# Linear attention into an MoE layer on one core: q, k and x transposed by DMA instead of on TensorE

## The chip, the core and the metric

The kernel runs on one core of a Trainium2 chip. The core has TensorE (PE, matmuls; its weight loads are counted apart as PEld), VectorE (DVE), ScalarE (ACT), GpSimd (POOL) and SyncE (SP). Each engine works through its own instructions in order, and waits on semaphores for the others. DMAs are issued from the queues of SP and POOL and run on 16 DMA engines that all queues share. TensorE writes to PSUM, and what it wrote there is read by DVE or ACT; SBUF is the large on-chip memory.

The metric is the device time of one execution, in microseconds. Before the change three runs gave 448.0, 448.2 and 449.42 us, median 448.2.

## The reference

The inputs are q, k and v of shape (8 batches, 8 heads, 576 positions, 64), a feature matrix w_phi (64 x 128), and the weights w_in (512 x 2048) and w_out (2048 x 512), all float32.

```python
def phi(x):
    proj = np.einsum('bhsd,df->bhsf', x, w_phi)
    proj = proj - np.max(np.abs(proj), axis=-1, keepdims=True)
    return np.concatenate([np.exp(proj), np.exp(-proj)], axis=-1)
q_p, k_p = (phi(q), phi(k))
kv = np.einsum('bhsf,bhsd->bhfd', k_p, v)
z = np.sum(k_p, axis=2)
num = np.einsum('bhsf,bhfd->bhsd', q_p, kv)
den = np.einsum('bhsf,bhf->bhs', q_p, z)[..., None] + 1e-06
attn = num / den
# heads side by side: x has 4608 rows of 512
h = x @ w_in
g = np.where(h > 0.0, h, np.exp(np.minimum(h, 0.0)) - 1.0)
out = g @ w_out
```

## The kernel before

**Attention.** The work is cut into 16 quads: quad i is batch i // 2 and four of its eight heads. For a quad, 128 partitions hold positions; the 576 positions of a head are 4 x 128 plus a tail of 64, and the tails of two heads share one block, so that k of a quad is nine blocks of 128 x 128 in bf16. `transposes` (lines 127 to 148) turns the nine blocks of k, and then those of q, on TensorE: eight into one PSUM tile `tr` (line 135), copied to `kT` or `qT` at once (line 137), and the tail block into `trt` (lines 139, 140). `project` (line 156) multiplies kT or qT by w_phi and takes the largest absolute value on DVE (line 164); `k_head` takes the exponentials `EK` on ACT (line 177); `k_scale` and `v_scaled` build `vs`, the scaled v, on POOL (lines 188 to 202; on DVE for quad 1); `q_features` makes `Eq` on ACT (lines 211, 219); `kv` accumulates kv (lines 252, 264); `out_head` and `out_tail` make numerator and denominator in `tot` (lines 285 to 324); `divide` writes `x` in bf16 on POOL (line 333). `x_out` (lines 340 to 362) transposes x on TensorE, again nine blocks, and copies them on DVE to `xT`, the tile of the batch's MoE chunk, and to `xT_tail`, which gathers the tails of all batches.

**MoE.** The 4608 rows are nine chunks of 512: chunk b is the main part of batch b and needs the x of quads 2b and 2b+1; chunk 8 (`B`) is made of all tails. A chunk is 16 units of `mm1` (four matmuls into `ph`, line 389, then exp on ACT, line 397, a subtraction of one on POOL, line 399, and min/max into `gT` on DVE, line 402) and four units of `mm2` (16 matmuls into `po`, line 410, a copy to `o_sb` on ACT, line 418, and a store issued from SP, lines 421 and 425). `o_sb` has two buffers.

**Order of the work.** The main loop has slots n = 0 to 16. `slot_steps(n)` mixes the steps of quad n (`new`: k, scale, q, vs, qf), of quad n - 1 (`old`: kv, out, x) and the transposes of quad n + 1 (`nxt["tr"]`), in an order written by hand. After each step MoE units are put in until their number reaches `due`, which grows evenly: 136 units over 14.5 slots, from slot 2.5 on (line 558). `chunk_ready` opens a chunk; for chunks 1 to 7 that is the last step of an even slot, right behind `old["x"]`. Units that are left at the end run behind the loop, with chunk 8. The instructions of an engine then stand in an order that a scheduler derives from this one; an instruction of a later step can stand ahead of one of an earlier step on the same engine.

**Loads and queues.** k and q come in from HBM through POOL's queue, cast to bf16 on the way (line 104 of `load_main`, and `load_tails`); v comes through SP's queue from batch 1 on. Tiles k_b, q_b and v_b have two buffers each, one for a batch; kT, qT, EK and Eq have two buffers each, one for a quad. Weights w_in and w_out come through POOL's queue in the first slots. SP's queue thus holds v loads and output stores, in order; a DMA that waits for its semaphores holds all behind it.

Of the kernel before, what the change touches and what calls it, by code (L numbers as in the profile page):

```python
# [9 lines left out]
BF16 = mybir.dt.bfloat16  # L10
# [12 lines left out]
def kernel(  # L23
# [10 lines left out]
    nc = tc.nc  # L34
    P = 128

    B, H, S, D = q.shape
# [6 lines left out]
    N_CT = DM // P  # L44
    N_JT = DFF // P
    CHUNK = 512
# [3 lines left out]
    TAIL = S - MAIN  # L50
# [3 lines left out]
    consts = ctx.enter_context(tc.tile_pool(name="consts", bufs=1))  # L54
# [13 lines left out]
    ident = consts.tile([P, P], BF16)  # L68
# [15 lines left out]
            out=w_out_sb[:, jt:jt + 2, :], in_=w_out_r[:, jt:jt + 2, :]  # L84
        )

    xT_tail = consts.tile([P, N_CT, B * TAIL], BF16)
    xTs = {B: xT_tail}


    HW = NT * D
# [31 lines left out]
    def attention_steps(i):  # L123
        b, qd = divmod(i, 2)
        st = states[i] = {}

        def transposes(n):
            src = kqv[b][n]
            m0, t0 = 4 * qd * HW, BW + qd * P
            nm = ("kT", "qT")[n]  # L130
            dst = st[nm] = work.tile([P, NS, P], BF16, name=nm)
            tr = apsum.tile([P, 8, P], BF16, name="tr", tag="ap")
            for j in range(8):
                o = m0 + j * P
                nc.tensor.transpose(tr[:, j, :], src[:, o:o + P], ident)  # L135
            copy = nc.scalar.copy if n == 1 and b == 0 else nc.vector.tensor_copy
            copy(dst[:, 0:8, :], tr)  # L137
            trt = apsum.tile([P, P], BF16, name="trt", tag="ap")
            nc.tensor.transpose(trt, src[:, t0:t0 + P], ident)
            copy(dst[:, 8, :], trt)  # L140
            if n == 0:
                st["m_k"] = small.tile([P, 2 * NS], FP32, name="m_k")
                st["EK"] = work.tile([P, 4, 2, NT * F], BF16, name="EK")
                st["EKt"] = work.tile([P, 2, 2 * F], BF16, name="EKt")
            else:
                st["m_q"] = small.tile([P, 2 * NS], FP32, name="m_q")
                st["Eq"] = work.tile([P, 2, 2, 2, 4 * P], BF16, name="Eq")
                st["Eqt"] = work.tile([P, 2, 2 * P], BF16, name="Eqt")
# [189 lines left out]
                )  # L338

        def x_out():  # L340
            tr = apsum.tile([P, 8, P], BF16, name="tr", tag="ap")
            for j in range(8):
                nc.tensor.transpose(
                    tr[:, j, :],
                    st["x"][:, j].rearrange("p c d -> p (c d)"),
                    ident,
                )
            if qd == 0:
                xTs[b] = xtp.tile([P, N_CT, CHUNK], BF16, name="xT")
            nc.vector.tensor_copy(  # L350
                xTs[b][:, 2 * qd:2 * qd + 2, :],
                tr.rearrange("p (s t) n -> p s (t n)", s=2),
            )
            trt = apsum.tile([P, 2, TAIL], BF16, name="trt", tag="ap")
            nc.tensor.transpose(
                trt.rearrange("p s j -> p (s j)"),
                st["x"][:, 8].rearrange("p c d -> p (c d)"),
                ident,
            )
            nc.vector.tensor_copy(  # L360
                xT_tail[:, 2 * qd:2 * qd + 2, b * TAIL:(b + 1) * TAIL], trt
            )

        def each(f, *a):
            return lambda: f(*a)
# [18 lines left out]
    def mm1(ch, jt):  # L384
        if jt == 0:
            gTs[ch] = gpool.tile([P, N_JT, CHUNK], BF16, name="gT")
        ph = mpsum.tile([P, CHUNK], FP32, name="ph", tag="mp")
        for ct in range(N_CT):
            nc.tensor.matmul(  # L389
                ph,  # L390
                w_in_sb[:, ct, jt * P:(jt + 1) * P],
                xTs[ch][:, ct, :],
                start=(ct == 0),
                stop=(ct == N_CT - 1),
            )
        e_sb = moesm.tile([P, CHUNK], FP32, name="e_sb")
        nc.scalar.activation(e_sb, ph, ACT.Exp)  # L397
        u_sb = moesm.tile([P, CHUNK], BF16, name="u_sb")
        nc.gpsimd.tensor_scalar(  # L399
            u_sb, e_sb, -1.0, 1.0, op0=ALU.add, op1=ALU.mult  # L400
        )
        nc.vector.scalar_tensor_tensor(  # L402
            gTs[ch][:, jt, :], u_sb, 0.0, ph, op0=ALU.min, op1=ALU.max
        )
# [47 lines left out]
    def chunk_ready(ch):  # L452
        first.extend((ch, jt) for jt in range(N_JT))

    def slot_steps(n):
        old, new, nxt = quads.get(n - 1), quads.get(n), quads.get(n + 1)
        if n == 0:
            return (
                new["k"] + new["scale"] + new["q"][:2] + nxt["tr"] + new["q"][2:]
                + new["vs"] + new["qf"]  # L460
            )
        if n == 1:
            steps = new["k"] + new["scale"] + old["kv"]
            for j in range(5):
                steps += new["q"][j:j + 1] + old["out"][j:j + 1]
                steps += new["vs"][j:j + 1]
            return steps + new["vs"][5:] + new["qf"] + nxt["tr"]
        if n == 2:

            return (  # L470
                old["kv"] + quads[0]["x"] + old["out"] + old["x"]
                + [lambda: chunk_ready(0)]
                + new["k"] + new["scale"] + new["q"] + new["vs"] + new["qf"]
                + nxt["tr"]
            )
        none = {"k": [], "q": [], "scale": [], "qf": [], "vs": []}
        new = new or none
        kk, qq, vv = new["k"], new["q"], new["vs"]
        steps = (
            old["kv"][:1] + kk[:1] + old["kv"][1:] + kk[1:3]  # L480
            + old["out"][:1] + kk[3:4] + old["out"][1:2] + kk[4:]
            + new["scale"]
            + old["out"][2:3] + vv[:1] + qq[:1] + old["out"][3:4] + vv[1:2]
            + qq[1:2] + old["out"][4:] + vv[2:3]
            + qq[2:4] + vv[3:4] + qq[4:]
        )
        for j in range(5):
            steps += new["qf"][j:j + 1] + vv[4 + j:5 + j]
        if nxt:
            steps += nxt["tr"]  # L490
        steps += old["x"]
        if n % 2 == 0:
            steps.append(lambda: chunk_ready(n // 2 - 1))
        return steps

    make_identity(nc, ident)
    for b in range(2):
# [18 lines left out]
    def load_kq(b):  # L516
        return [
            lambda f=f, n=n: f(n)
            for n in range(2)
            for f in (  # L520
                lambda n: load_main(nc.gpsimd, n, b, 0, 8),
                lambda n: load_tails(nc.gpsimd, n, b),
            )
        ]

    def load_v(b, after=None):
        if after is not None:
# [11 lines left out]
        f()  # L539
    extra = w_in_loads[3:] + load_kq(1) + w_out_loads  # L540

    UNITS = 136
    done = 0
    for n in range(NQ + 1):
        if n + 1 < NQ:
            quads[n + 1] = attention_steps(n + 1)
        if n % 2 == 0 and 1 < n // 2 + 1 < B:
            alloc_batch(n // 2 + 1)
            extra += load_kq(n // 2 + 1)
            load_v(n // 2 + 1)  # L550
        steps = slot_steps(n)
        for j, step in enumerate(steps):
            step()
            if n == 1 and step is quads[1]["scale"][0]:
                load_v(1, after=states[1]["em"][:, 0, 0:1])
            if extra and ((n == 0 and j > 16) or n == 1 or j % 3 == 2):
                extra.pop(0)()
            due = (n + (j + 1) / len(steps) - 2.5) * UNITS / 14.5
            while done < due and (first or second):
                moe_unit()  # L560
                done += 1
    chunk_ready(B)
    while first or second:
        moe_unit()
# [30 lines left out]
```

## Time and profile before

| | |
|---|---|
| median of three runs | 448.2 us |
| the profiled execution's own time | 447.22 us |
| span of its records | 445.4 us |
| mean granted TensorE clock | 0.977 |
| TensorE busy | 396.4 us, 89% |
| DVE busy | 283.8 us, 64% |
| ACT busy | 264.6 us, 59% |
| POOL busy | 243.8 us, 55% |
| HBM read / written | 36.77 MB / 9.44 MB |

The profile is of one execution. Its times count from the start of the span. Busy time is the union of an engine's instructions, and matmuls overlap, so a busy TensorE need not be at its peak. In the slices each digit is the busy share of 1/40 of the span in tenths; PEclk is the granted clock, DMA the mean busy share of the 16 DMA engines. A group is named by its line, engine and operation, with output <- inputs. In a list of waits, "A <- B" says that A's engine stood idle until B had ended. Some records of matmuls are missing: of 576 each, 556 of line 410 and 542 of line 389 are there.

### The profile page before, as it was taken

To read this page: it belongs to the slowest core of one execution; us is meant where nothing else is said; L and a number is where in the kernel's file an instruction comes from. 1 tells how busy PE (TensorE), PEld (TensorE's weight loads), DVE (VectorE), ACT (ScalarE), POOL (GpSimd) and SP (SyncE) were. 2 spreads that over 40 slices of the span, in tenths; PEclk is the share of its full clock that TensorE was granted. 3 is DMA by queue.
4 is the path that set the end of the run, shared out by engine and by line. 5 is a ranking of instruction groups with operands and counts; after the bars stand their busy time and mean duration, and the time that the engine had idled before them with its cause. 6 is when DMAs were issued, how large, how long until landed. Compare 5 with 4: busy or idle time off the path is not lost.

```text
span 445.4 us, 8463 instructions
## 1 busy us (share of the span) xinstructions
PE 396.4 (89%) x3194; PEld 221.5 (50%) x3248; DVE 283.8 (64%) x602; ACT 264.6 (59%) x585; POOL 243.8 (55%) x355
## 2 busy tenths in 40 slices
PE   3668659999999998999899989999889998999995
PEld 2445336555555455646465646554545454444442
DVE  2675859954897279927994589656978564443420
ACT  2854288745966487737775578566767733344331
POOL 9676078744694279446945494618283725342320
PEclk9955999999999999999999999999999999999999
DMA  8999929312830191119121912100000010011013
GB/s 135 215 186 233 227 28 106 107 49 58 98 107 25 71 108 55 55 71 132 23 86 56 145 28 83 48 25 25 2 0 25 25 42 32 24 50 47 25 47 71
DMA packets 45081, 33.12 MB, mean 74 GB/s; under 512 B 13904, under 2 KB 39632, under 8 KB 45040
## 3 DMA queue, kind: packets, MB, share of 16 engines
q0 software_dynamic: 28544, 14.82, 24.8%
q1 hardware_dynamic: 16496, 17.76, 12.9%
q8 instruction: 25, 0.41, 0.4%
q14 instruction: 16, 0.13, 0.1%
HBM read 36.77 MB, written 9.44 MB: 104 GB/s over the span
## 4 chain that ended last, share of the span: by engine, by line
PE 54%; ACT 14%; DVE 13%; POOL 11%; issue 5%; DMA 1%; POOLq 0%; ACTq 0%
PE po L410 24%; PE ph L389 13%; ACT EK L177 5%; ACT Eq L219 5%; POOL u_sb L399 4%; POOL vs L202 4%; PE pk L156 4%; DVE gT L402 4%; PE pkv L252 3%; PE tr L135 3%; ACT e_sb L397 2%; POOL x L333 2%; DVE m_q L164 2%; DVE m_k L164 2%; PE pn L285 2%
## 5 line engine op out<-in xcount | busy, mean ns | idle before, releaser
L399 POOL TENSOR_SCALAR u_sb<-e_sb 128x512 bf16<-128x512 f32 x144 | 87.7, 616 | 114.8 <-ACT e_sb L397 104.6
L389 PE MATMUL ph<-xT,w_in_sb 128*128 128x512 bf16 x480 | 130.5, 379 | 8.8 <-DVE gT L402 6.9
L410 PE MATMUL po<-w_out_sb,gT 128*128 128x512 bf16 x556 | 134.5, 379 | 0.8
L402 DVE SCALAR_TENSOR_TENSOR gT<-u_sb,ph 128x512 bf16<-128x512 bf16 x144 | 96.8, 681 | 56.8 <-POOL u_sb L399 56.2
L397 ACT ACTIVATE e_sb<-ph 128x512 f32<-128x512 f32 x144 | 86.4, 636 | 35.5 <-PE ph L389 33.0
L202 POOL TENSOR_TENSOR vs<-v_b,em 128x512 bf16<-128x512 f32 (+1 forms) x90 | 73.0, 830 | 27.4 <-ACT em L188 27.3
L410 PEld LDWEIGHTS <-gT 128*128 128x128 bf16 x576 | 54.5, 98 | 56.6 <-issue 1.0
L389 PEld LDWEIGHTS <-w_in_sb 128*128 128x128 bf16 x576 | 52.2, 97 | 52.3 <-issue 14.2
L219 ACT ACTIVATE Eq<-pq 128x512 bf16<-128x512 f32 x128 | 65.9, 639 | 15.5 <-PE pq L211 15.4
L177 ACT ACTIVATE EK<-pk 128x512 bf16<-128x512 f32 x128 | 68.0, 630 | 11.5 <-DVE m_k L164 11.2
L418 ACT COPY o_sb<-po 128x512 f32<-128x512 f32 x36 | 21.3, 593 | 83.9 <-PE po L410 66.7
L164 DVE TENSOR_REDUCE m_k<-pk 128x4 f32<-128x512 f32 (+1 forms) x80 | 49.0, 632 | 19.1 <-PE pk L156 18.7
L164 DVE TENSOR_REDUCE m_q<-pk 128x4 f32<-128x512 f32 (+1 forms) x80 | 49.4, 626 | 16.2 <-PE pk L156 16.0
L285 PEld LDWEIGHTS <-Eq 128*128 128x128 bf16 x512 | 30.2, 99 | 26.3 <-issue 10.5
L333 POOL TENSOR_TENSOR x<-tot,rec 128x576 bf16<-128x576 f32 x30 | 33.8, 1145 | 10.0 <-DVE rec L330 9.8
L285 PE MATMUL pn<-kv,Eq 128*128 128x65 bf16 x512 | 34.6, 196 | 4.9 <-DVE tot L295 1.1
L156 PE MATMUL pk<-w_phi_both,qT 128*128 128x256 bf16 x144 | 29.1, 288 | 4.4 <-ACT EK L177 2.2
L156 PE MATMUL pk<-w_phi_both,kT 128*128 128x256 bf16 x144 | 28.5, 287 | 3.2 <-ACT Eq L219 1.9
L295 DVE TENSOR_TENSOR tot<-pn,w 128x260 f32<-128x260 f32 x64 | 27.1, 424 | 5.6 <-PE pn L285 5.2
L137 DVE COPY kT<-tr 128x1024 bf16<-128x1024 bf16 x16 | 11.0, 688 | 29.8 <-PE tr L135 29.8
L301 DVE TENSOR_TENSOR tot<-tot,pn 128x260 f32<-128x260 f32 x64 | 26.7, 418 | 0.3
L252 PE MATMUL pkv<-vs,EK 128*128 128x65 bf16 x512 | 22.9, 198 | 1.9 <-ACT EK L177 1.2
(62 smaller groups left out, 358.8 us busy)
## 6 DMA issues: line engine op xcount, KB each, us to landing
out_dram<-o_sb SPq DMA_DIRECT2D x32, 256.0 KB, 2.3
v_b<-in_v_dram SPq DMA_DIRECT2D x7, 1024.0 KB, 5.7
k_b<-in_k_dram POOLq DMA_DIRECT2D x7, 512.0 KB, 6.9
q_b<-in_q_dram POOLq DMA_DIRECT2D x7, 512.0 KB, 7.7
w_in_sb<-in_moe_w_in_dram POOLq DMA_DIRECT2D x8, 256.0 KB, 7.8
w_out_sb<-in_moe_w_out_dram POOLq DMA_DIRECT2D x8, 256.0 KB, 11.9
v_b<-in_v_dram POOLq DMA_DIRECT2D x2, 512.0 KB, 6.4
out_dram<-o_sb SPq DMA_DIRECT2D x8, 128.0 KB, 2.4
```

What stands on the lines that cost most here:

```text
L156: nc.tensor.matmul(pk[:, 2 * j:2 * j + 2, :].rearrange("p a b -> p (a b)"), xT[:, 2 * hh + j, :], w_phi_rhs, start=True, stop=True,)
L164: nc.vector.tensor_reduce(m[:, o:o + NT] if hh < 4 else m[:, NS - 1::NS], pk[:, 0:2 * n, :], axis=AX.X, op=ALU.max, apply_absolute_value=True,
L177: nc.scalar.activation(dst, pk, ACT.Exp, scale=1.0 - 2.0 * sg)
L202: eng.tensor_tensor(st["vs"][:, sg, r, 0:D], kqv[b][2][:, o:o + n * D].rearrange("p (n d) -> p n d", d=D), st["em"][:, sg, r, None].to_bro ...
L219: nc.scalar.activation(st["Eq"][:, par, c, sg, :], pq, ACT.Exp, scale=1.0 - 2.0 * sg)
L285: nc.tensor.matmul(pt[:, t, :], st["Eq"][:, par, c, sg, o:o + P], st["kv"][:, s, c, sg, :], start=True, stop=True,)
L333: eng.tensor_tensor(st["x"][:, :, c, :], st["tot"][:, r, 0:D], rec[:, r, None].to_broadcast((P, NS, D)), op=ALU.mult,)
L389: nc.tensor.matmul(ph, w_in_sb[:, ct, jt * P:(jt + 1) * P], xTs[ch][:, ct, :], start=(ct == 0), stop=(ct == N_CT - 1),)
L397: nc.scalar.activation(e_sb, ph, ACT.Exp)
L399: nc.gpsimd.tensor_scalar(u_sb, e_sb, -1.0, 1.0, op0=ALU.add, op1=ALU.mult)
L402: nc.vector.scalar_tensor_tensor(gTs[ch][:, jt, :], u_sb, 0.0, ph, op0=ALU.min, op1=ALU.max)
L410: nc.tensor.matmul(po, gT[:, jt, tt * P:(tt + 1) * P], w_out_sb[:, jt, :], start=(jt == 0), stop=(jt == N_JT - 1),)
```

## The change

Three things change.

- `transposes` keeps TensorE for quad 0 alone. For quads 1 to 15 it issues two transposing DMAs from SP for k and two for q, SBUF to SBUF: one of 128 x 1024 elements for eight blocks, one of 128 x 128 for the tail block.
- `x_out` keeps TensorE for batch 0 (quads 0 and 1). For quads 2 to 15 it issues two transposing DMAs from SP. `xT_tail` gets another layout, with the two tails of a quad next to each other, and the first matmuls of chunk 8 read it with a step.
- In `slot_steps` the transposes of quad n + 1 move from the end of slot n to its first third (in slot 1 ahead of the q features, in slot 2 behind the scaling of k). A chunk is opened in the odd slot that follows its last x, after four steps, and not at the end of the even one; chunk 7 is opened behind the loop. `due` is 20 units over the 2.6 slots up to 5.1, and then 120 units over 11.9 slots.

```diff
-    xT_tail = consts.tile([P, N_CT, B * TAIL], BF16)
-    xTs = {B: xT_tail}
+    xT_tail = consts.tile([P, 2, B, 2, TAIL], BF16)
+    xTs = {}
@@ transposes
-            tr = apsum.tile([P, 8, P], BF16, name="tr", tag="ap")
-            for j in range(8):
-                o = m0 + j * P
-                nc.tensor.transpose(tr[:, j, :], src[:, o:o + P], ident)
-            copy = nc.scalar.copy if n == 1 and b == 0 else nc.vector.tensor_copy
-            copy(dst[:, 0:8, :], tr)
-            trt = apsum.tile([P, P], BF16, name="trt", tag="ap")
-            nc.tensor.transpose(trt, src[:, t0:t0 + P], ident)
-            copy(dst[:, 8, :], trt)
+            if i == 0:
...
+            else:
+                nc.sync.dma_start_transpose(
+                    out=dst[:, 0:8, :], in_=src[:, m0:m0 + 8 * P]
+                )
+                nc.sync.dma_start_transpose(out=dst[:, 8, :], in_=src[:, t0:t0 + P])
@@ x_out
+            if qd == 0:
+                xTs[b] = xtp.tile([P, N_CT, CHUNK], BF16, name="xT")
+            main = xTs[b][:, 2 * qd:2 * qd + 2, :].rearrange(
+                "p s (t n) -> p (s t) n", n=P
+            )
+            tail = xT_tail[:, qd, b].rearrange("p s j -> p (s j)")
+            x = st["x"].rearrange("p n c d -> p (n c d)")
+            if b > 0:
+                nc.sync.dma_start_transpose(out=main, in_=x[:, 0:8 * P])
+                nc.sync.dma_start_transpose(out=tail, in_=x[:, 8 * P:])
+                return
...
@@ mm1
-                xTs[ch][:, ct, :],
+                xTs[ch][:, ct, :] if ch < B else xT_tail[:, ct // 2, :, ct % 2, :],
@@ slot_steps
-            return steps + new["vs"][5:] + new["qf"] + nxt["tr"]
+            return steps + new["vs"][5:] + nxt["tr"] + new["qf"]
...
-                + new["k"] + new["scale"] + new["q"] + new["vs"] + new["qf"]
-                + nxt["tr"]
+                + new["k"] + new["scale"] + nxt["tr"] + new["q"] + new["vs"]
+                + new["qf"]
...
+        ready = []
+        if n % 2 == 1 and n > 3:
+            ready = [lambda: chunk_ready((n - 3) // 2)]
         steps = (
-            old["kv"][:1] + kk[:1] + old["kv"][1:] + kk[1:3]
+            old["kv"][:1] + kk[:1] + old["kv"][1:] + kk[1:2]
+            + ready + kk[2:3] + (nxt["tr"] if nxt else [])
...
-        if nxt:
-            steps += nxt["tr"]
-        steps += old["x"]
-        if n % 2 == 0:
-            steps.append(lambda: chunk_ready(n // 2 - 1))
-        return steps
+        return steps + old["x"]
@@ main loop
-    UNITS = 136
...
-            due = (n + (j + 1) / len(steps) - 2.5) * UNITS / 14.5
+            at = n + (j + 1) / len(steps)
+            due = (at - 2.5) * 20 / 2.6 if at < 5.1 else 20 + (at - 5.1) * 120 / 11.9
...
+    chunk_ready(B - 1)
     chunk_ready(B)
```

More of the change, by code (lines that the diff above doesn't have):

```diff
@@ L131, in transposes @@
             dst = st[nm] = work.tile([P, NS, P], BF16, name=nm)
-            tr = apsum.tile([P, 8, P], BF16, name="tr", tag="ap")
-            for j in range(8):
-                o = m0 + j * P
-                nc.tensor.transpose(tr[:, j, :], src[:, o:o + P], ident)
-            copy = nc.scalar.copy if n == 1 and b == 0 else nc.vector.tensor_copy
-            copy(dst[:, 0:8, :], tr)
-            trt = apsum.tile([P, P], BF16, name="trt", tag="ap")
-            nc.tensor.transpose(trt, src[:, t0:t0 + P], ident)
-            copy(dst[:, 8, :], trt)
+            if i == 0:
+                tr = apsum.tile([P, 8, P], BF16, name="tr", tag="ap")
+                for j in range(8):
+                    o = m0 + j * P
+                    nc.tensor.transpose(tr[:, j, :], src[:, o:o + P], ident)
+                copy = nc.scalar.copy if n == 1 else nc.vector.tensor_copy
+                copy(dst[:, 0:8, :], tr)
+                trt = apsum.tile([P, P], BF16, name="trt", tag="ap")
+                nc.tensor.transpose(trt, src[:, t0:t0 + P], ident)
+                copy(dst[:, 8, :], trt)
+            else:
[3 more added lines that the diff above has]
+                nc.sync.dma_start_transpose(out=dst[:, 8, :], in_=src[:, t0:t0 + P])
             if n == 0:
@@ L340, in x_out @@
         def x_out():
+            if qd == 0:
[9 more added lines that the diff above has]
+                return
             tr = apsum.tile([P, 8, P], BF16, name="tr", tag="ap")
             for j in range(8):
[L343 to L362, printed above, removed]
+                nc.tensor.transpose(tr[:, j, :], x[:, j * P:(j + 1) * P], ident)
+            nc.vector.tensor_copy(main, tr)
+            trt = apsum.tile([P, P], BF16, name="trt", tag="ap")
+            nc.tensor.transpose(trt, x[:, 8 * P:], ident)
+            nc.vector.tensor_copy(tail, trt)
         def each(f, *a):
```

## The prediction

> **What bounds the kernel now.** I read the page's busy line and slices first, then a table of busy time by stage, then the order of time on TensorE in one slot, then the waits, then the DMA lines.
>
> The page, parts 1 and 2 (busy time; the span in 40 slices of 11.1 us, in tenths):
>
> ```profile
> PE 396.4 (89%) x3194; PEld 221.5 (50%) x3248; DVE 283.8 (64%) x602; ACT 264.6 (59%) x585; POOL 243.8 (55%) x355
> ...
> PE   3668659999999998999899989999889998999995
> ...
> PEclk9955999999999999999999999999999999999999
> DMA  8999929312830191119121912100000010011013
> ```
>
> From the seventh slice on TensorE is at 8 or 9 tenths; before that, nothing is. So there are two stages: a start of 66 us, and a filled part. The table by stage of time (columns: stretch, its length, then busy us and count for PE, PEld, DVE, ACT, POOL, then clock, DMA share, GB/s):
>
> ```profile
> 66.00:372.00 306.00, 287.23 (x2543) 164.63 (x2588) 221.50 (x482) 202.34 (x457) 180.57 (x256) 1.00 0.30 60
> 200.35:220.48 20.13, 18.75 (x178) 10.99 (x179) 16.93 (x37) 15.02 (x34) 14.95 (x23) 1.00 0.56 74
> ```
>
> In the filled part TensorE is busy 94%, the next engine (DVE) 72%. That part is what an instruction taken from TensorE shortens. TensorE in order of time in one slot (start, us, what; an end is modelled, so starts are what to subtract):
>
> ```profile
> 200.35 0.61 PE L135 MATMUL tr<-ident,k_b 128*128 128x128 bf16 x8
> 200.80 0.22 PE L139 MATMUL trt<-ident,k_b 128*128 128x128 bf16 x1
> 200.85 1.03 PE L389 MATMUL ph<-xT,w_in_sb 128*128 128x512 bf16 x4
> ...
> 202.39 0.61 PE L343 MATMUL tr<-ident,x 128*128 128x128 bf16 x8
> 202.84 0.22 PE L355 MATMUL trt<-ident,x 128*128 128x128 bf16 x1
> ```
>
> A set of nine transposes takes the engine from 200.35 to 200.85, 0.50 us or 56 ns each, not nine times the 219 ns that the groups give for one: they overlap. There are three sets to a slot. The x transposes start at 85.01 us and, twelve slots on, at 355.58: a slot is 22.5 us.
>
> What TensorE waited for (waits, longest first; us, times, longest):
>
> ```profile
> PE ph L389 <- DVE gT L402: 6.9, 11, 2.2
> ...
> PE tr L135 <- DVE kT L137: 3.1, 5, 1.4
> ...
> PE tr L343 <- POOL x L333: 1.7, 2, 1.5
> ```
>
> The queue that the transposes move to (page, parts 3 and 6, and the waits on SP):
>
> ```profile
> q1 hardware_dynamic: 16496, 17.76, 12.9%
> ...
> out_dram<-o_sb SPq DMA_DIRECT2D x32, 256.0 KB, 2.3
> v_b<-in_v_dram SPq DMA_DIRECT2D x7, 1024.0 KB, 5.7
> ...
> SPq L103 <- POOL vs L202: 115.9, 5, 36.6
> ```
>
> SP issues little and mostly stands waiting. One of its packets takes 0.129 x 16 x 445.4 us / 16496 = 55.7 ns of an engine.
>
> **What the Trainium skill says.** "VectorE: DVE Perf Modes", section "The three transpose paths", gives 390 ns for a 128x128 transpose on TensorE and 1309 ns by DMA; the trace has 219 ns for one on TensorE and 56 ns in a row, so at least the first is a latency. "Advanced Engine Details and Errata", section "X-Bar Transpose (TRN2)", says a transposing DMA is as fast as an ordinary one; no run here shows it yet. "DMA: Bandwidth & Descriptors", section "Anatomy of one DMA", gives about 2 us fixed for a DMA, mostly completion; the 2.3 us of the 256 KB stores agrees. The same page, section "Issuing engines are not separate DMA queues", says that all queues share the 16 engines; the saturated start agrees (DMA 9 in the slices, landings of 5 to 12 us).
>
> **The change, part by part.**
>
> *Removed.* Fifteen k sets, fifteen q sets and fourteen x sets leave TensorE: 44 sets, 396 transposes. In the filled part lie those of k and q from quad 3 on (26) and x (14): 40 x 0.505 us = 20.2 us. The other four (quads 1 and 2) ran in the start, at half clock for a part, 1.1 to 1.3 us a set (14.62 to 15.60 for the first); the chain there runs mostly through ACT, so of 5 us I count 2. With them go 44 pairs of copies out of PSUM, 0.69 + 0.21 us each on DVE (one on ACT: 1.01 + 0.27), 39 us of DVE in all. They end in waits of TensorE: 3.1 on kT, 0.5 + 0.3 on xT, 0.2 on qT, 1.7 on x: 5.8 us, of which I count 4, since some will be met by the next instruction. The rest of the copies I cost at nothing: DVE is not the bound, TensorE's matmuls hide it.
>
> *Added.* 44 pairs of transposing DMAs on SP, one of 256 KB and one of 32 KB. The trace shows none. Call D what a pair takes of the queue. Lowest: at 261 GB/s, which the skill states for such DMAs ("DMA: Bandwidth & Descriptors", section "Latency and other measured facts"), 0.295 MB take 1.1 us. Highest: nine times 1309 ns, 11.8 us, if that price is per block and nothing overlaps. Nearest row: 128 rows x 9 groups are 1152 packets of 256 B, at 55.7 ns over 16 engines 4.0 us. I take 4.0 as an estimate, and 2 us more to landing; 1.1 and 11.8 stay for the range.
>
> *What waits for them.* In the built order kT of quad n+1 stands on SP over one slot before its first use (30 us of TensorE work), qT about as long: a landing of 6 us is hidden, and buffers of two quads leave the room. The x of an odd quad is the short one: between its last division and the first matmul of the chunk the built order has 9.3 us of TensorE work (instructions of that order times the spacings of this trace: the remaining second-half matmuls, pq, kv), because the chunk is opened a few steps into the next slot. 6 us fit; without that cover they would cost 6 us x 7 chunks. The last chunk has 32 matmuls, 6.9 us, against division (1.2 us DVE, 2.25 POOL) and 4.5 to 6 us: up to 2 us late, where before stood 1.5; I count +2. At the start kT of quad 1 can go out when the second half of k_b is in (at the latest 14.6) into 16 full engines, so D counts twice: 2 + 8 = 10 us, against a first use at 20.7: 3 to 4 us late, less what ACT and TensorE no longer do there; +2.
>
> *Moved.* Behind the transposes on SP stand output stores and v loads, and in front of some stand v loads that wait for POOL's vs. The stores feed two o_sb buffers, so a late one stops ACT's copy, then TensorE's po. Stores come some 4 us apart in the second half of a chunk; SP's issue of one plain DMA is 0.33 us, and a pair at 4 us in a slot with three leaves over half the queue free: nothing.
>
> *The pace.* Chunk 0 gets 2.6 slots, the others 10.1 units a slot instead of 9.4; 40 units remain at the end instead of 44. Units are TensorE work in either place: nothing.
>
> *Sum* against the profiled span: 445.4 - 20.2 - 2 - 4 + 2 + 2 = 423.2. The profiled execution took 447.2, so 1.8 lie around the span: 425.0. The median of the runs shown is 1.0 above the profiled one: **426 us**.
>
> **The rivals.**
> - *The transposing queue becomes the bound* (slower). Place: SP's queue from slot 3 on, three pairs a slot. A slot would need some 22 us, so it decides from D = 7.5 us. Each us beyond costs 3 us a slot over 13 slots, 39 us. At D = 9, 426 + 58 = 484; at 11.8, 40 pairs from 34 us on are 506 us, and two chunks of 128 matmuls (16 take 3.45 us in the trace's chain, so 27.6) behind them give 561, up to 600 with rigid slots. For it: the 1309 ns; the loads already hold 0.40 of the engines from 66 to 260 us, and D = 4 adds 12 of 22, 0.55. Against: the 261 GB/s, and 56 ns a packet.
> - *x arrives late at each chunk.* With landings of 12 us, 3 us x 7 = 21 us, the whole gain: 447. For it: plain loads of 1 MB land in 5.7 us and up to 20 us when crowded. Against: x has an otherwise short queue.
> - *The time saved becomes gaps on TensorE.* The waits on gT show that first-half units are tied to DVE and POOL; if half the gain turns into such waits, 436. Against: DVE loses 39 us of copies at the same time.
> - That transposes don't leave TensorE is excluded by the built order.
>
> **How the numbers follow.** 0.56 for 426 (its own range 417 to 437), 0.08 for half a gain, 0.07 for x late (0.02 faster, 0.04 same, 0.01 slower), 0.29 for the queue as the bound. The line between change and no change is 0.3%, 446.9 to 449.5, what this kernel's measurement can tell. Faster 0.66, same 0.04, slower 0.30. Of the queue's 0.29, half lies above 500 and perhaps 0.03 of the first case below 416: the range is 416 to 500.
>
> **What will show it.** Right: TensorE's tr groups down to quad 0 and x of the first batch, slot about 22 us with more units in it, pairs landing within 6 us, no wait of ph for an xT DMA above a few us in all. Wrong: slices of PE at 5 or 6 with DMA at 9 throughout, SP transposes back to back, and waits of pk on kT's DMA. It fails if D is above 7.5 us.

## The result and the profile after

The changed kernel takes 487.8 us (median of four runs, 484.3 to 492.5) against 448.2 us before: ratio 1.085, 95% interval 1.079 to 1.091. It is slower by 39.6 us where the prediction had it faster by 22. The time lies inside the stated range (416 to 500), but in the part of it that stood for another mechanism, so that is luck.

The profiled execution is the slowest of the four (492.5 us, span 490.7; before 447.2 and 445.4) and counts as a slow run, which the ratio, one of means, leaves out; its granted clock, 0.907, is close to the 0.911 and 0.912 of the two runs of 488 us. So the spans differ by 45.3 us, some 6 more than the medians. Busy line, TensorE's slices, granted clock and DMA from the page of the kernel after, as shown of before:

```profile
PE 384.9 (78%) x2804; PEld 202.8 (41%) x2852; DVE 249.1 (51%) x516; ACT 261.9 (53%) x583; POOL 244.4 (50%) x355
...
PE   3317632866897779885997589989988998999996
...
PEclk9855858798699979997998979999999999999999
DMA  9999999329554654377334646162221301110113
```

TensorE has 390 fewer recorded matmuls, yet its busy time fell by 11.5 us only, and the time in which it does nothing grew from 49.0 to 105.8 us: +56.8 - 11.5 = 45.3. The busy time by stage says where (stretch, length, then busy us and count of PE, PEld, DVE, ACT, POOL, then clock, DMA share, GB/s; the DMA share adds up the times of packets and can pass 1):

```profile
0.00:66.00 66.00, 28.40 (x251) 17.66 (x252) 26.87 (x64) 22.56 (x53) 34.87 (x55) 0.74 1.27 172
...
66.00:110.00 44.00, 25.52 (x188) 13.91 (x191) 22.70 (x44) 24.47 (x56) 23.06 (x35) 0.81 0.75 93
110.00:200.00 90.00, 74.21 (x570) 39.81 (x578) 44.57 (x93) 51.26 (x119) 43.51 (x61) 0.89 0.61 111
200.00:290.00 90.00, 68.92 (x522) 36.04 (x531) 50.73 (x107) 49.84 (x115) 52.70 (x75) 0.91 0.54 98
```

Before, TensorE was busy for 40.65, 41.67, 85.20 and 85.01 us in the same stretches, at 0.84, 1.00, 1.00 and 1.00 of the clock. So TensorE is less busy by 12 us up to 66 us, by 16 up to 110 and by 27 from there to 290; a part of that is the work taken away. How late the kernel is can be read from the start of POOL's division of x. For quad 2 it comes at 111.0 us instead of 82.7, for quad 5 at 183.8 instead of 146.4, for quad 11 at 337.4 instead of 284.0: 28, 37 and 53 us late. The last q load is issued at 281.1 us, and at the end of the span 45 are left. What TensorE and POOL waited for (the list of waits: us in all, times, longest; at "issue" the profile shows nothing that was waited for):

```profile
PE ph L392 <- DVE gT L405: 37.5, 15, 7.5
...
PE pk L163 <- DMA kT<-k_b: 24.4, 2, 15.6
POOL k_b L104 <- DMA qT<-q_b: 22.5, 1, 22.5
...
POOL q_b L104 <- DMA qT<-q_b: 20.8, 3, 7.5
...
POOL q_b L104 <- issue: 7.9, 2, 7.6
```

The waits on the copies to kT and on x are gone as planned. In their place TensorE waits 37.5 us for gT (6.9 before) and twice for kT, 15.6 us at quad 1 and 8.8 at quad 2. The lines of POOL are the key: line 104 is the *load* of a later batch's k or q. It writes a buffer that a transposing DMA still reads, and POOL stands at it. (At the one long wait of a k load, 22.5 us, the list names the qT that landed last; kT of quad 3, which does read that buffer, had landed 1 us before, at 77.8.) The order of time in one such place, kernel after (start, us, what; the bracket is the idle time before it and what ended it):

```profile
164.24 1.26 SPq L356 DMA_TRANSPOSE xT<-x  x1
...
165.55 1.22 SPq L357 DMA_TRANSPOSE xT_tail<-x  x1
...
166.81 1.29 SPq L114 DMA_DIRECT2D v_b<-in_v_dram  x2
...
168.21 1.28 SPq L144 DMA_TRANSPOSE qT<-q_b  x1
...
169.53 1.23 SPq L147 DMA_TRANSPOSE qT<-q_b  x1
...
172.45 0.96 POOL L104 DMA_DIRECT2D q_b<-in_q_dram  x1 [6.47 <-DMA qT<-q_b]
173.45 1.21 POOL L402 TENSOR_SCALAR u_sb<-e_sb 128x512 bf16<-128x512 f32 x2
174.12 1.29 DVE L405 SCALAR_TENSOR_TENSOR gT<-u_sb,ph 128x512 bf16<-128x512 bf16 x2 [5.00 <-POOL u_sb L402]
...
174.85 0.59 PE L392 MATMUL ph<-xT,w_in_sb 128*128 128x512 bf16 x1 [5.18 <-DVE gT L405]
```

Read it downwards. SP issues xT, its tail, two v loads, qT and its tail, one after the other, 1.2 to 1.3 us for a transposing one. Only when the qT tail has landed, at 172.4, does POOL issue its q load. POOL has stood at it since 166.0, with the subtraction for `u_sb` (line 402) behind it, though its input is ready; gT needs `u_sb`, and TensorE stands for 5.2 us. Between 170 and 175 us it is busy for 0.14 us. The Trainium skill, "TensorE: Matmul & The Clock Gate", section "Part 1: The HAM clock gate (the "warmup" mystery)", says that an idle TensorE falls to half clock after about 3.4 us and needs as much work to come back; this trace agrees, with 0.50 and 0.74 in the first 4 us after the gap and 1.00 from then on (granted clock, same columns):

```profile
175.00:177.00 2.00, 2.00 (x13) 0.92 (x12) 1.67 (x4) 0.00 (x0) 1.99 (x4) 0.50 1.31 161
177.00:179.00 2.00, 2.00 (x18) 0.89 (x16) 0.32 (x1) 0.60 (x1) 2.00 (x4) 0.74 1.12 114
179.00:185.00 6.00, 5.92 (x30) 2.86 (x30) 4.97 (x13) 1.68 (x4) 4.79 (x8) 1.00 0.12 44
```

The queue that was feared is not the bound (page, parts 3 and 6, and the median time to landing of the transposing DMAs):

```profile
q1 hardware_dynamic: 70000, 30.75, 30.6%
...
out_dram<-o_sb SPq DMA_DIRECT2D x32, 256.0 KB, 2.3
...
kT<-k_b SPq DMA_TRANSPOSE x30, 3.1
...
xT<-x SPq DMA_TRANSPOSE x14, 3.2
```

The queue has 53504 more packets, 44 pairs of 1216, and (0.306 x 490.7 - 0.129 x 445.4) x 16 = 1483 us more of engine time: 27.7 ns a packet, 2.1 us of all 16 engines a pair, as an estimate that puts the whole difference down to the pairs. Output stores land in 2.3 us as before.

### The profile page after: what moved, and what is told of

It reads as the page before. It is cut to its first block, busy times and chain, and to the rows that moved or that the text cites. A ratio compares the mean times of both kernels' runs of the same rounds, so it can differ in the third digit from the quotient of the medians.

```text
span 490.7 us, 7744 instructions
## 1 busy us (share of the span) xinstructions
PE 384.9 (78%) x2804; PEld 202.8 (41%) x2852; DVE 249.1 (51%) x516; ACT 261.9 (53%) x583; POOL 244.4 (50%) x355
## 4 chain that ended last, share of the span: by engine, by line
PE 41%; POOL 16%; DMA 13%; DVE 11%; issue 9%; ACT 9%; SPq 1%; POOLq 0%; ACTq 0%; DVEq 0%
PE po L413 24%; DMA kT<-k_b 10%; PE ph L392 10%; POOL u_sb L402 6%; POOL vs L209 5%; ACT EK L184 5%; DVE gT L405 4%; PE pk L163 3%; ACT Eq L226 2%; DMA qT<-q_b 2%; DVE tot L302 2%; DVE m_k L171 2%; POOL x L340 2%; DVE m_q L171 2%; ACT e_sb L400 1%
## 5 line engine op out<-in xcount | busy, mean ns | idle before, releaser
L392 PE MATMUL ph<-xT,w_in_sb 128*128 128x512 bf16 x481 | 138.1, 394 | 39.7 <-DVE gT L405 37.5
L413 PE MATMUL po<-w_out_sb,gT 128*128 128x512 bf16 x559 | 136.0, 387 | 1.8 <-DVE gT L405 1.1
L400 ACT ACTIVATE e_sb<-ph 128x512 f32<-128x512 f32 x144 | 88.2, 647 | 52.7 <-PE ph L392 49.3
L184 ACT ACTIVATE EK<-pk 128x512 bf16<-128x512 f32 x128 | 71.6, 664 | 37.2 <-DVE m_k L171 36.8
L392 PEld LDWEIGHTS <-w_in_sb 128*128 128x128 bf16 x576 | 53.7, 100 | 72.3 <-issue 35.6
L413 PEld LDWEIGHTS <-gT 128*128 128x128 bf16 x576 | 55.7, 99 | 62.7 <-issue 3.1
L421 ACT COPY o_sb<-po 128x512 f32<-128x512 f32 x36 | 21.1, 586 | 97.0 <-PE po L413 80.3
L163 PE MATMUL pk<-w_phi_both,kT 128*128 128x256 bf16 x144 | 29.8, 301 | 27.2 <-DMA kT<-k_b 24.4
L292 PE MATMUL pn<-kv,Eq 128*128 128x65 bf16 x512 | 35.1, 199 | 11.9 <-DVE tot L302 7.4
L163 PEld LDWEIGHTS <-kT 128*128 128x128 bf16 x144 | 13.3, 106 | 35.9 <-DMA kT<-k_b 24.8
## 6 DMA issues: line engine op xcount, KB each, us to landing
w_out_sb<-in_moe_w_out_dram POOLq DMA_DIRECT2D x8, 256.0 KB, 13.2
```

The lines of the kernel that those rows point to most:

```text
L163: nc.tensor.matmul(pk[:, 2 * j:2 * j + 2, :].rearrange("p a b -> p (a b)"), xT[:, 2 * hh + j, :], w_phi_rhs, start=True, stop=True,)
L184: nc.scalar.activation(dst, pk, ACT.Exp, scale=1.0 - 2.0 * sg)
L292: nc.tensor.matmul(pt[:, t, :], st["Eq"][:, par, c, sg, o:o + P], st["kv"][:, s, c, sg, :], start=True, stop=True,)
L392: nc.tensor.matmul(ph, w_in_sb[:, ct, jt * P:(jt + 1) * P], xTs[ch][:, ct, :] if ch < B else xT_tail[:, ct // 2, :, ct % 2, :], start=(ct ...
L413: nc.tensor.matmul(po, gT[:, jt, tt * P:(tt + 1) * P], w_out_sb[:, jt, :], start=(jt == 0), stop=(jt == N_JT - 1),)
```

## The experiments

All kernels compute the whole result. Times are medians. Ratios are of means, to the kernel before, measured beside each, with the 95% interval. "Start" stands for quads 1 to 3, "loads" for POOL's loads of k and q.

**The start alone.** k and q of quads 1 to 3 go back to TensorE.

```diff
-            if i == 0:
+            if i < 4:
```

> The changed kernel, but k and q of quads 0 to 3 (batches 0 and 1) are transposed on TensorE; only quads 4 to 15 use the DMAs for them. Theory (a crowded start plus held POOL loads later): by the x of quad 2 the changed kernel is 28 us behind the kernel before; these 28 us come back nearly whole, the stops of TensorE for gT in the batches with loads stay: 488 - 26 = about 462 us. Rival A (the new order and pace are at fault): the time stays near 485. Rival B (the transposing DMAs slow everything they run beside, in the middle as in the start): 475 to 485.

466.5 us, 1.042 (1.038 to 1.045). 21.3 of the 39.6 us come back. POOL's waits at its q loads stay (21.1 + 6.8 us), TensorE's for gT are 30.7 in place of 37.5.

**A third buffer for k_b and q_b**, so that a load needn't wait for the batch before, alone and with the start on TensorE:

```diff
-            stage.tile([P, BW + 4 * D], BF16, name="k_b"),
-            stage.tile([P, BW + 4 * D], BF16, name="q_b"),
+            stage.tile([P, BW + 4 * D], BF16, name="k_b", bufs=3),
+            stage.tile([P, BW + 4 * D], BF16, name="q_b", bufs=3),
```

> The changed kernel with three buffers instead of two for k_b and q_b, so that POOL's loads of a batch need not wait for the transposes of the batch before last. Theory: POOL's waits for transposing DMAs (22.5 us in the start, 7 us a batch later) go, and with them TensorE's waits for gT (37.5 us to about 10); the late kT of quads 1 and 2 (15.6 and 8.8 us of TensorE) stays: 488 - 30 = about 458 us. Rival A: no change, 485 or more. Rival B: POOL's loads start earlier and crowd more: 485 or more.

> Both edits: quads 0 to 3 transposed on TensorE, and three buffers for k_b and q_b. Theory: both losses gone, what stays is the gain of the transposes taken from TensorE in the filled part (36 sets of 0.5 us less the copies' waits): 426 to 434 us. Rival A: 455 or more. Rival B: 445 to 465, since the DMAs still run beside everything.

476.6 us, 1.063 (1.057 to 1.069), and 459.3 us, 1.025 (1.022 to 1.029): both far above what the theory expected. The waits of the first of the two tell why:

```profile
POOL q_b L104 <- DMA qT<-q_b: 13.7, 2, 7.8
POOL q_b L104 <- issue: 10.7, 3, 7.4
```

The loads moved a batch earlier with the buffer: the k load of batch 3 goes out at 53.2 us instead of 78.8. So they stand at the head of POOL again, in front of the same transposes: at 116.0 us it is the q load of batch 5 that has waited 7.8 us for the last qT of batch 2, where in the changed kernel it was the one of batch 4, at 120.8. A buffer gives a load room; it does not say where in POOL's order the load stands.

**The order alone.** Every transpose on TensorE, with the order, pace and chunk opening of the change.

```diff
-            if i == 0:
+            if i < 16:
@@ x_out
-            if b > 0:
+            if b > 7:
```

> The changed kernel with every transpose on TensorE: only the new order of steps, the later opening of chunks, the pace and the layout of xT_tail are left. Theory: the order costs nothing by itself, 445 to 453 us. Rival A (order and pace are at fault): 470 to 490. Rival B: as the theory.

465.0 us, 1.038 (1.034 to 1.042): with TensorE's transposes the new order costs 16.8 us, a miss (445 to 453 was expected). One more thing differs. The changed source copies a qT that comes from TensorE on ACT, so here ACT makes all 16 of these copies, 1.06 us each, where before DVE made 14 of them; what this costs was not separated. The waits name the place of a large part:

```profile
PE tr L361 <- POOL x L340: 16.7, 7, 2.8
```

Before, this wait was 1.7 us. There the transposes of the next quad stood between the division of x and x's own transposes. The new order takes them away, and TensorE meets x unfinished. That cost is not in the changed kernel, where x isn't transposed on TensorE after batch 0; it says that the order fits only the DMA form.

**The crowded start.** The weight loads, and the k and q loads of batch 1, are held until quad 0's q weights are made, to give kT of quad 1 free DMA engines. Else it is the changed kernel.

```diff
+    def hold():
+        t = states[0]["w"]
+        nc.gpsimd.tensor_copy(w_in_sb[:, :, 0], t[:, 0:N_CT])
...
-    for f in w_in_loads[:3]:
-        f()
-    extra = w_in_loads[3:] + load_kq(1) + w_out_loads
+    extra = [hold] + load_kq(1) + w_in_loads + w_out_loads
...
-            if extra and ((n == 0 and j > 16) or n == 1 or j % 3 == 2):
+            if extra and n and (n == 1 or j % 3 == 2):
```

> The changed kernel, but POOL's loads of w_in, w_out and of k and q of batch 1 are held back until quad 0's tile w exists (some 20 us), so that quad 1's transposing DMAs meet emptier engines. Theory C (the transposes of the start are late because their many 256 B packets take turns with POOL's large loads): kT of quad 1 lands within 8 us of its issue instead of 20.7, and TensorE's wait for it falls from 15.6 us to under 4. Rival D (a transposing DMA that is the first of its kind, or whose issue stands behind another, is slow whatever runs beside it): it still lands after 15 us or more. The whole time may go either way, since the weights come 10 us later: 470 to 490.

488.6 us, 1.088 (1.085 to 1.092): no gain. The theory of the crowded start holds: the large DMA of kT of quad 1 lands in 4.4 us instead of 20.7, and TensorE no longer waits for it. But a wait on x of quad 0 (9.9 us) and one of 12.5 us at POOL's k load take its place; what was held back has to pass later, and kT of quad 2 now takes 17.0 us. POOL's waits for qT remain at 20.9 us.

**The loads held by hand.** One-column writes on POOL into k_b and q_b ahead of the loads of batches 2 to 7, which need the k weights `em` of the quad before; the loads can't be put earlier than that. With the start on TensorE.

```diff
+        def gate(n):
+            for o in (0, BW):
+                nc.gpsimd.tensor_copy(kqv[b][n][:, o:o + 1], after)
+        hold = [lambda: (gate(0), gate(1))] if after is not None else []
-        return [
+        return hold + [
...
-            extra += load_kq(n // 2 + 1)
+            extra += load_kq(n // 2 + 1, states[n - 1]["em"][:, 0, 0:1] if n else None)
```

> The kernel with quads 0 to 3 on TensorE (466.5 us), and in it POOL's loads of k and q of batches 2 to 7 get a small write on POOL ahead that needs em of the quad before, so that they can't stand in POOL's queue ahead of that. Theory (a load that waits for the transposing DMAs of its buffer holds POOL's subtraction, that DVE's gT, and that TensorE): POOL's waits for transposing DMAs (28 us) fall below 8, TensorE's wait for gT from 30.7 to some 10 us; 466 - 20 = 446 us, 440 to 452. Rival E (TensorE waits for gT because the order and the pace put first-half units too close together): gT waits stay above 25 us and the time at 460 or more.

446.9 us, 0.996 (0.995 to 0.998), as expected: 19.6 us from a few small writes that take no work away. POOL's waits for transposing DMAs are gone, TensorE's for gT fall from 30.7 to 18.0 us (some 10 were expected).

**The order of before under the DMA form** (start on TensorE, no gate), to see whether the later opening of chunks is what covers x:

```diff
-            + ready + kk[2:3] + (nxt["tr"] if nxt else [])
...
+        if nxt:
+            steps += nxt["tr"]
+        steps += old["x"]
+        if n % 2 == 0:
+            steps.append(lambda: chunk_ready(n // 2 - 1))
...
-            at = n + (j + 1) / len(steps)
-            due = (at - 2.5) * 20 / 2.6 if at < 5.1 else 20 + (at - 5.1) * 120 / 11.9
+            due = (n + (j + 1) / len(steps) - 2.5) * 136 / 14.5
```

> The kernel with quads 0 to 3 on TensorE (466.5 us) with the order of steps, the opening of chunks and the pace of the kernel before; the DMAs stay. Prediction's step (x is covered only because the chunk opens later): x's landing is then exposed at each chunk, some 6 us x 7, but the order's own cost of up to 16 us goes: 466 + 20 to 30 = 485 to 495. Rival E (the new order costs 16 us by itself, as with all transposes on TensorE): 450 us.

467.5 us, 1.042 (1.037 to 1.046): no different from 466.5, a miss. TensorE waits 6.0 us in all for xT's DMA. With POOL's waits in place (23.0 + 8.9 us) the order makes no difference that can be measured.

**The gate in the kernel before**, the edit of the gate above:

> The kernel before with the same small write ahead of POOL's loads of k and q. It waits 22.7 us on POOL for transposes too, but TensorE waits for gT only 6.9 us: theory 444 to 449 us. Rival E: no change either.

472.6 us, 1.053 (1.050 to 1.056), a miss: the gate costs the old kernel 24 us. Its loads now stand ahead of x's division on POOL, and TensorE needs x at once:

```profile
PE tr L343 <- POOL x L333: 16.3, 6, 3.9
```

**Which part of the DMA form carries the gain.** The gated kernel (446.9) with k and q all on TensorE, and with x all on TensorE:

```diff
-            if i < 4:
+            if i < 16:
```

```diff
-            if b > 0:
+            if b > 7:
```

> The gated kernel (446.9 us) with every k and q transposed on TensorE again and only x by DMA; the full result is computed. If TensorE's removed work is what the DMA form is worth, 24 sets of nine transposes come back (batches 2 to 7, four quads' worth per batch of k and q), 24 x 0.505 = 12 us, and the time is 457 to 461 us. If the gain comes from x alone (a transposing DMA for x frees TensorE from waiting for POOL's division, and k and q on TensorE cost only gaps), the time stays at 445 to 450. In both, no load on POOL waits for a transposing DMA, since none reads k_b or q_b.

> The gated kernel with x transposed on TensorE in every batch and only k and q by DMA from batch 2 on; the full result is computed. TensorE gets 14 sets back, 14 x 0.505 = 7 us; and in the order of the change nothing stands between x's division and its transposes, which with x on TensorE cost 16.7 us of waits in the kernel that changed only the order. Theory: both come, 446.9 + 7 + 8 to 16 = 462 to 470 us. Rival: the k and q transposes are the harmful part (queue, POOL), the gate has removed their harm, and x on TensorE costs its 7 us alone: 452 to 456.

454.4 us, 1.012 (1.010 to 1.015), between the two expectations: the 12 us of k and q work cost 7.5 (all copies of qT are on ACT here too). And 468.7 us, 1.046 (1.044 to 1.048), as the theory had it: x on TensorE in this order costs 21.8 us for 7 us of work, with TensorE waiting for x again (22.9 us).

**Where the load stands.** The gate ahead of the q loads alone, and both loads held one quad longer, to `em` of the even quad of their own slot, and then one issue at each step:

```diff
-        hold = [lambda: (gate(0), gate(1))] if after is not None else []
+        hold = [lambda: gate(1)] if after is not None else []
```

```diff
-            extra += load_kq(n // 2 + 1, states[n - 1]["em"][:, 0, 0:1] if n else None)
+            held = n // 2 + 1
...
+            if n and held and step is quads[n]["scale"][0]:
+                extra += load_kq(held, states[n]["em"][:, 0, 0:1])
+                held = 0
-            if extra and ((n == 0 and j > 16) or n == 1 or j % 3 == 2):
+            if extra and (n > 1 or (n == 0 and j > 16) or n == 1 or j % 3 == 2):
```

> The gated kernel with the gate ahead of the q loads alone, so the k loads go as early as POOL lets them. The full result is computed. If only the wait for qT (20 to 22 us in all) matters, since kT's DMA stands first in its pair and lands earlier, the time is 445 to 448. If a load at the head of POOL that waits for any transposing DMA is the harm, k's loads wait again for kT, u_sb comes late, TensorE's wait for gT goes from 18 back towards 25 or more, and the time is 452 to 460.

> The gated kernel with the loads of the next batch's k and q held one quad longer, to the k weights of the even quad of their own slot, and then issued one at each step. The full result is computed. Theory: POOL's waits are already gone in the gated kernel, so nothing more is to be had, and 446 to 449 us comes out, as long as k lands before its transposing DMA. If the place matters still (POOL's issue work ahead of x), 440 to 444. If the loads come too late, kT waits for k, TensorE waits for kT once per batch, 3 us or more each: 460 and over.

451.7 us, 1.007 (1.005 to 1.009): leaving k's loads free costs 4.8 us, between the two expectations and nearer to the second. But POOL waits at them for TensorE's last k transposes of the start (8.6 us, once), not for kT's DMA, and the wait for gT rises by 1.8 us only, so by which way the 4.8 us come isn't shown. The later loads give 441.9 us, 0.985 (0.984 to 0.987), the fastest kernel of the study; page and waits:

```profile
PE 383.2 (87%) x2906; PEld 203.3 (46%) x2906; DVE 253.5 (58%) x522; ACT 264.9 (60%) x589; POOL 246.6 (56%) x379
...
PEclk9958897999799999999999999999999999999999
```

```profile
PE po L413 <- DVE gT L405: 8.8, 10, 1.9
...
PE ph L392 <- DVE gT L405: 5.9, 12, 1.1
```

**The later loads alone, in the changed kernel.** The start stays as the change has it; against the kernel with the later loads:

```diff
-            if i < 4:
+            if i == 0:
```

> The changed kernel with only the later loads of the next batches' k and q (held to the k weights of the even quad of their own slot), the start left as the change has it, kT and qT of quads 1 to 3 by DMA. The full result is computed. Start and later loads were worth 21.3 us (487.8 to 466.5) and 24.7 us (466.5 to 441.9) one after the other. If they are two separate causes they add, and the time is 487.8 - 24.7 = 463, 460 to 467 us. If the late start also caused a part of POOL's waits (lateness passed on), the two overlap and the time is 450 to 457; if the loads can't be freed while the start is late, it is 475 or more.

447.5 us, 0.999 (0.997 to 1.001): below all three expectations. The later loads alone bring back 40.3 us, the whole loss to within what can be measured. The waits of this kernel:

```profile
POOL k_b L521 <- ACT em L195: 17.9, 3, 16.1
...
PEld L163 <- DMA kT<-k_b: 12.4, 1, 12.4
PE pk L163 <- DMA kT<-k_b: 12.3, 1, 12.3
...
PE po L413 <- DVE gT L405: 8.8, 10, 1.9
```

The wait for kT of quad 1 is still there, nearly as long. It costs 5.6 us (447.5 against 441.9): x of quad 2 is divided at 89.7 us here and at 83.7 with the start on TensorE, and the spans end 6.3 us apart. With the early loads the same edit was worth 21.3 us, x of quad 2 at 111.0 against 87.0. So the start's lateness was not a second cause of that size.

Where do the 40.3 us lie? From x of quad 2 to x of quad 11 the kernel before takes 201.3 us, the changed one 226.5, the one with the start on TensorE 224.8, and this one 202.0. So some 24 us are lost in the filled part, whether the start is late or not. A rival is that the later loads collide less with other transfers. It fails there: the DMA share in that stretch is higher with the later loads (0.65) than in the changed kernel (0.54). What fits is the place of the loads in POOL's order, which the order of time at 172 us shows at work.

The other 21 us arise before x of quad 2, and there two things go together. The early k load of batch 3 stood at the head of POOL for 22.5 us, until 78.8 us, because SP's transposes of quads 2 and 3 were late. And the loads of batch 2 went out from 51.9 us on, beside kT of quad 2, which took 24.2 us to land; now they go out from 66.0 us on, and the DMA share from 40 to 80 us is 1.05 instead of 1.36. Which of the two cost how much is not shown. That POOL stands is no harm by itself: the gate stands there for 16.1 us too (first line above).

**The later loads in the kernel before, and the old order with the later loads** (the control for the best kernel; and the question of x's cover again, with nothing else late):

> The kernel before, everything transposed on TensorE, with the same later loads: the control for the best kernel so far (441.9 us). The full result is computed. If the later loads only repair what the DMA form broke, the time is 446 to 450, as before, and the DMA form is truly worth 6 us. If POOL's waits for TensorE's transposes in the kernel before (22.7 us on its k loads) cost it as much as they cost the changed kernel, the time is 436 to 443 and the DMA form is worth nothing. If the loads still stand ahead of x on POOL, as with the earlier gate, it is 460 and over.

> The kernel with k, q and x by DMA from quad 4 and the later loads (441.9 us), but with the order, the pace and the chunk opening of the kernel before. The full result is computed. With POOL's waits in place the order made no difference (466.5 and 467.5). If it makes none now either, 440 to 444. If x's landing (2.4 to 3.2 us) has to be covered by the later opening, it shows once nothing else is late: division and landing, 3 to 5 us in each of 7 chunks, 455 to 475, with TensorE's waits for xT in the trace.

456.4 us, 1.018 (1.014 to 1.023): the later loads cost the old kernel 8 us, so the gain of the best kernel (441.9) isn't theirs alone. 451.2 us, 1.006 (1.003 to 1.009): once POOL's waits for transposing DMAs are gone the order and pace do matter, 9.4 us, and the waits of that kernel show x's landing as one part of it:

```profile
PE ph L392 <- DMA xT<-x: 12.1, 5, 4.4
```

The kernels side by side (us; in the rows "DMA transposes" the k and q of quads 1 to 3 are on TensorE; the 465.0 has the copies of qT on ACT):

| | early loads | later loads |
|---|---|---|
| TensorE transposes, old order | 448.2 | 456.4 |
| TensorE transposes, new order | 465.0 | not run |
| DMA transposes, old order | 467.5 | 451.2 |
| DMA transposes, new order | 466.5 | 441.9 |
| DMA also in the start, new order (the change) | 487.8 | 447.5 |

The steps differ from column to column and from row to row: the parts of the change depend on each other, and a time below that of the kernel before came only with all of x, k and q by DMA, the new order, and the loads held.

## Why the prediction was wrong

**The step that failed is the list of what waits, in the parts "What waits for them" and "Moved".** The first weighs only the readers of the results, TensorE's use of kT, qT and x; the second lists what stands behind the transposes on SP, and costs it at nothing. Both leave out who waits for a transposing DMA to *end*: the loads that overwrite its source, k_b or q_b, which POOL issues, with POOL's own arithmetic behind them. With the DMA form TensorE's wait for gT went from 6.9 to 37.5 us. Holding the loads takes 40.3 us off the changed kernel, and nothing else in it is altered.

Before, these loads waited too, for TensorE's last k transposes:

```profile
POOL k_b L103 <- PE trt L139: 22.7, 5, 7.4
```

That cost little, for TensorE had other work at that time. In the longest of these waits nearly half of it was second-half matmuls (start, us, what):

```profile
148.33 3.62 PE L410 MATMUL po<-w_out_sb,gT 128*128 128x512 bf16 x15
151.78 1.03 PE L211 MATMUL pq<-qT,w_phi_both 128*128 128x512 bf16 x4
...
156.13 0.98 POOL L103 DMA_DIRECT2D k_b<-in_k_dram  x1 [7.43 <-PE trt L139]
```

In the four long waits of the kernel before, 22.3 us, TensorE was busy for 21.5. In the changed kernel it was busy for 8.0 of the 22.5 us up to 78.8 (where it waited for kT of quad 2 too), for 4.9 of the 7.5 up to 120.8 and for 2.9 of the 6.5 up to 172.4.

**Removed, 20.2 us plus 4 of waits plus 2 in the start.** The instructions went, 390 recorded matmuls. The time did not follow: busy fell by 11.5. A part is clock: the changed kernel with the later loads runs the same TensorE instructions in 378.4 us of busy time instead of 384.9, at a clock of 0.944 instead of 0.907. In the best kernel, 38 of the 40 sets gone from the filled part and the end, busy falls by 13.2 and idle grows by 6.6; 6.3 us are left (ratio 0.985). From x of quad 2 to x of quad 11 it takes 201.5 us, as the kernel before (201.3), with TensorE idle for 18.3 us instead of 10.2; its gain lies behind that. So even with the loads held the sum (22 us) was too high by some 15. The rival "the time saved becomes gaps" (436) comes nearest, and the reason it gave, first-half units tied to DVE and POOL, fits the waits on gT; that this is all of it is argued, not shown.

**D, 4.0 us, and a landing of 6 us.** Both too high: 2.1 us of the engines a pair, within its bounds (1.1 to 11.8), and 3.2 us to landing for the large DMA of a pair. The nearest row misled, since packets of loads and stores took 55.7 ns and these take 27.7; the former carried 1077 bytes on average, the latter 243. The fixed 2 us came about right, for the small DMA landed in 2.4 us, though the section cited for it is on DMAs issued from GpSimd and these go from SP. The rival of the transposing queue as the bound, with 0.29, is excluded: D would have had to be over 7.5. The slower outcome came, and not for its reason, so the chance given to "slower" is no credit to the argument; "it fails if D is above 7.5" named the wrong test.

**x is covered because chunks open later.** Right: with the changed order no wait on xT shows among the longer ones, and in the old order with later loads there are 12.1 us of them.

**The start, kT of quad 1 "3 to 4 us late", +2.** The mechanism was right, D doubled by full engines; the size was off. kT of quad 1 took 20.7 us to land and that of quad 2 24.2, not 10, and TensorE waited 15.6 and again 8.8 us. With the later loads the DMA form in the start costs 5.6 us; with the early ones it cost 21.3.

**The pace, nothing.** Not so in general: with later loads the old order and pace cost 9.4 us; which of the two was not separated.

**Open.** Why the later loads cost the kernel before 8 us was not settled; the earlier gate hurt it by way of x (16.3 us of waits), and the later one shows no such single wait. How the 21 us of the start divide between POOL's order and the fuller DMA engines is open too.

## What to carry to other kernels

When a consumer of a buffer moves from an engine to a DMA queue, list what waits for it to let the buffer go, on every queue: a reload at the head of an in-order engine that also computes passes each delay on to the arithmetic behind it, and it hurts where another engine needs that arithmetic just then. An extra buffer did not mend it here, because the load moved up with it; its place in the order did, and a small write into the buffer that needs a late value fixes the place. Try the suspected cure on the old kernel too: here both gates made that one slower, which is how the gain of the DMA form could be told from theirs.

## What the runs showed of the hardware

- A transposing DMA held SP for 1.2 to 1.3 us to issue (median), a plain store for 0.33 to 0.35 us; one in the start, with the DMA engines full, held it for 13.8 us.
- The 256 KB DMA of a pair landed in 3.2 us and the 32 KB one in 2.4 (medians); in the start those of kT took 20.7 and 24.2 us, and 4.4 for quad 1 once the other loads were held. Plain output stores landed in 2.3 us (median).
- At 27.7 ns a packet a pair takes 2.1 us of the 16 engines, 140 GB/s. That is below the 309 GB/s that the plain loads and stores of this queue reach by the same reckoning (17.76 MB in 0.129 of 445.4 us). The Trainium skill, "Advanced Engine Details and Errata", section "X-Bar Transpose (TRN2)", calls transposing DMAs as fast as regular ones; for blocks of this shape the runs don't bear that out. Packets of 243 bytes stand against packets of 1077 here, so what is due to their size and what to the transposing is not separated.
- After a gap of 5 us TensorE worked for some 4 us at 0.50 to 0.74 of its clock.
